# Sums of v's blocks made by accumulating transfers, two halves split in one instruction, and a row's transfers planned longer

## The chip, the cores and the metric

The kernel runs on one core of a Trainium2 chip. The metric is the device time of one execution in microseconds; lower is better. The engines of the core are named as the profile names them: PE (matrix products; PEld is its weight load), DVE (vector), ACT (scalar functions), POOL (GpSimd, here used nearly only to issue transfers), SP (issues the other transfers).

## What is computed

Channel attention followed by a layer with an activation in between. For each of 4 batches, with 6080 rows and 256 channels:

```python
qn = q / (np.linalg.norm(q, axis=1, keepdims=True) + 1e-06)
kn = k / (np.linalg.norm(k, axis=1, keepdims=True) + 1e-06)
s = kn.transpose(0, 2, 1) @ qn / tau
a = np.exp(s - s.max(-1, keepdims=True))
a /= a.sum(-1, keepdims=True) + 1e-09
x = (v @ a).reshape(24320, 256)
h = x @ w_in                          # 256 -> 2048
g = np.where(h >= 1, h, np.where(h <= -1, 0.0, (h + 1) ** 2 / 4))
out = g @ w_out                       # 2048 -> 256
```

All inputs and the output are float32.

## The kernel before

The product a @ w_in is formed once for a batch ("W", in eight pieces of 256 hidden columns), so that the bulk of the work is h = v @ W and out = g @ w_out. The rows of a batch are cut into 6 pairs of blocks of 512 (the last two pairs: 496) rows. A **group** g is one batch b, one pair k and one of the 8 pieces i; there are 192 groups, and a pair of blocks is 8 groups long. Each product of 2 x 2 blocks is made with seven block products instead of eight: for that, v's blocks (b11, b12, b21, b22) are combined into four sums, T1 = b11 + b12, T2 = T1 + b22, T3 = b12 + b22 and T4 = T2 + b21, and used beside b11, b21 and b22. Every factor is split into a high and a low half in float32r, and a product is three matmuls (`mm3`): high x high, high x low, low x high.

`make_V` makes the seven factors of a pair of blocks while the pair before it is worked on: two loads from DRAM, four additions on DVE (`combo`), and for each factor a cast to the high half (ACT, or DVE) and a subtraction for the low half (DVE). `h_ops` makes the products of a group and, in four steps of `tile_ops`, the activation: two ACT instructions and one on DVE for each of the four blocks of h, in a buffer of the pool "u". `halves_of` then splits a block into halves in a buffer of the pool "g" (tiles g and x); in a third of the groups (`o_forms`) sums of the blocks are split instead.

While a batch is worked on, the statistics for the next one are gathered. `norms` turns them into reciprocal norms in the tile cols; those of the columns are needed as a row in every partition, so SP stores them to DRAM (row_d) and loads them back, spread over all partitions, into a tile y or y_mem. `softmax` multiplies with that row on DVE, takes the exponential on ACT, transposes on PE and splits the result into halves (eT); the pieces of W are products with eT (`make_W2`).

The order of all instructions is written by the kernel's own planner (`Order`): it places operations by estimated durations, due times and free buffers, computes from that plan how late each could be, adds a table of corrections (`BIAS`) and plans again. Each engine then runs its list in that order. For transfers the planner counts a landing time:

```python
if o.size:
    dma = max(dma, t + self.DMA_BEGIN) + o.size / self.BYTES
    o.end = dma + self.DMA_END
    if o.eng == "POOL":
        o.end = max(o.end, t + self.ADDED)
```

with DMA_BEGIN 1.0, DMA_END 3.0 and ADDED 6.0 us. Accumulating transfers are used before the change for the output alone (`outT`, from tiles y and y_mem, issued by POOL).

Of the kernel before, what the change touches and what calls it, by code (L numbers as in the profile page):

```python
# [56 lines left out]
L_ADDED = 6.0  # L57
SOON = 0.6


class Op:
    __slots__ = ("eng", "dur", "fn", "due", "deps", "gates", "bufs", "next", "count", "start", "end", "n", "size",
                 "alts", "psum", "plain", "tag", "bias", "placed", "late", "freed", "latest")


class Order:
# [7 lines left out]
    DMA_BEGIN, DMA_END, ADDED = 1.0, L_END, L_ADDED  # L74

# [19 lines left out]
    def op(self, eng, dur, fn, r=(), w=(), due=0.0, gates=(), size=0, other=None, psum=False, plain=False, tag=0):  # L95
# [3 lines left out]
        o.psum, o.plain = psum, plain  # L99
# [73 lines left out]
    def plan(self):  # L173
# [25 lines left out]
        while left:  # L199
# [132 lines left out]
def dve_us(n):  # L332
    return 0.067 + 0.00104 * n
# [6 lines left out]
def pool_us(n):  # L340
# [9 lines left out]
U = 32  # L350

EARLY = 7
POOL_DMA = 1.0
T_MAX = -0.5
T_HALF = -36.2
T_FORM = -18.6
T_V = 4.5
T_VS = 29.9
T_GRAM = 34.6
T_SQ = 31.6  # L360
T_W2 = -39.4
T_O = 10.9
T_SO = 20.8
T_P4 = 3.8
BIAS = {
    (48, 4): 0.9,
    (48, 6): -1.9,
    (49, 0): 1.5,
    (49, 2): 3.8,
    (49, 5): -5.5,  # L370
    (50, 4): 1.2,
    (50, 5): -3.2,
    (51, 0, 0): -1.0,
# [12 lines left out]
    (56, 0): -4.9,
    (56, 4): -0.9,
    (62, 0): 5.3,
    (67, 0, 0, 0): -0.3,
    (67, 1, 0, 1): 0.3,  # L390
    10: 0.3,
    14: -0.2,
    15: 3.4,
    16: 0.4,
    2: 1.8,
    21: 2.8,
    27: 0.8,
    32: 6.7,
    41: 0.6,
    42: -20.7,  # L400
    46: -1.7,
    5: -4.9,
    57: 3.1,
    6: -3.5,
    65: -25.5,
    7: -2.0,
    71: 0.7,
    72: 0.2,
# [16 lines left out]
V_SPREAD = 4.2  # L425
WARM = 8
STORE = 15
IN3 = False
WIN_DUE = 21.3
W_DUE = -57.1  # L430
# [3 lines left out]
V1 = 16.2  # L434
V1S = 3.8
# [6 lines left out]
def channel_attention_moe(ctx: ExitStack, tc: tile.TileContext, kq, kqT, vT, tau, w_in, w_out, outT):  # L442
# [44 lines left out]
    def slot2(j, h):  # L487
# [16 lines left out]
        "g": Pool([sb("g6", [2, TB], F32R), *[lambda j=j, h=h: slot2(j, h) for j in range(3) for h in range(2)]]),  # L504
        "w": Pool([w_mem[:, i * WSZ:(i + 1) * WSZ].rearrange("p (a j f) -> p a j f", a=2, j=NS) for i in range(4)]),
        "v": Pool([*[sb(f"v{i}", [2, TB], F32R) for i in range(8)], *[lambda h=h: slot2(3, h) for h in range(2)]], ordered=True),
        "t": Pool([sb(f"t{i}", [TB]) for i in range(2)], ordered=True),
        "raw": Pool([*[sb(f"raw{i}", [1024]) for i in range(4)], shared.tile([P, 1024], F32, name="raw4", tag="raw")]),
        "kqs": Pool([sb("kqs", [2, RT, 2, C], F32R)]),
        "u": Pool([sb(f"u{i}", [TB]) for i in range(6)]),  # L510
# [21 lines left out]
    pools["g"].held[1:] = [kq_all] * 6  # L532
# [712 lines left out]
```

## Time and profile before

| | |
|---|---|
| time, median of 3 runs | 2140.2 us (2139.72 to 2141.19) |
| the profiled execution | 2139.28 us, its span 2137.5 us |
| busy, share of the span | PE 99%, DVE 96%, ACT 89%, POOL 8% |
| matmul instructions in the trace | 9728 |
| mean granted clock of PE | 0.998 |
| moved by the transfer engines | 386.29 MB, mean 181 GB/s |

The time of an execution holds the span, from the first to the last instruction, and a little around it. Busy time adds up an engine's instructions without counting an overlap twice. The granted clock is that of PE as a share of 2.4 GHz.

### The profile page before, as it was taken

How to read it: one execution, taken by the hardware profiler on the slowest of the kernel's cores; microseconds unless marked ns; L12 is line 12 of the kernel's file. 1: busy time of each engine (PE TensorE's matmuls, PEld its weight loads, DVE VectorE, ACT ScalarE, POOL GpSimd, SP SyncE). 2: the span in 40 equal slices, each digit the busy share in tenths (PEclk: the TensorE clock that was granted, in tenths of full speed). 3: DMA queues.
4: the chain of work that ended last, by engine and by line, in shares of the span. 5: the costliest groups of instructions: out<-in, count | busy, mean ns of one | idle time of the engine just before them, and what ended most of it. 6: DMA issues, size and time to landing. Idle time of an engine off the chain costs nothing.

```text
span 2137.5 us, 29493 instructions
## 1 busy us (share of the span) xinstructions
PE 2119.1 (99%) x9728; PEld 1764.6 (83%) x9728; DVE 2044.2 (96%) x3648; ACT 1901.5 (89%) x3530; POOL 160.5 (8%) x188
## 2 busy tenths in 40 slices
PE   9999999999999999999999999999999999999999
PEld 8888888888888888888788888888878888888887
DVE  8999999999999999999999999999989999999995
ACT  7889999998999999998898999999979899889885
POOL 0000101001001010010100101001001010010010
PEclk9999999999999999999999999999999999999999
DMA  9755657666467576665737667666564654564551
GB/s 389 277 189 187 185 185 209 193 180 157 140 213 206 193 202 203 197 182 177 169 105 243 190 204 198 193 208 189 157 166 107 208 145 128 161 145 128 160 125 37
DMA packets 108075, 386.29 MB, mean 181 GB/s; under 512 B 12050, under 2 KB 27922, under 8 KB 104082
## 3 DMA queue, kind: packets, MB, share of 16 engines
q1 hardware_dynamic: 82578, 338.73, 45.8%
q0 software_dynamic: 25344, 45.69, 15.1%
q8 instruction: 76, 1.25, 0.2%
q14 instruction: 77, 0.63, 0.1%
HBM read 280.23 MB, written 104.14 MB: 180 GB/s over the span
## 4 chain that ended last, share of the span: by engine, by line
PE 88%; DVE 7%; DMA 2%; ACT 1%; issue 1%; SPq 0%; POOL 0%; DVEq 0%; ACTq 0%; POOLq 0%
PE bank L653 88%; DVE u L934 1%; DVE x L947 1%; DVE mh_mem L1138 1%; DMA y_mem<-row_d 1%; DMA raw<-kqT 1%; DMA raw<-vT 0%; DVE w_mem L794 0%; DVE bank L970 0%; DMA y<-row_d 0%; DVE v L889 0%; DVE mh_mem L974 0%; DMA kq<-kq 0%; ACT u L930 0%; DVE u L580 0%
## 5 line engine op out<-in xcount | busy, mean ns | idle before, releaser
L653 PE MATMUL bank<-v,w_mem 128*128 128x512 f32 (+1 forms) x3240 | 854.0, 390 | 8.7 <-DVE bank L970 8.1
L653 PE MATMUL bank<-x,wout 128*128 128x512 f32 (+1 forms) x3165 | 817.0, 388 | 0.0
L653 PEld LDWEIGHTS bank<-v,w_mem 128*128 128x128 f32 x3240 | 601.9, 188 | 141.3 <-DVE bank L970 14.1
L653 PEld LDWEIGHTS bank<-x,wout 128*128 128x128 f32 x3165 | 593.6, 188 | 118.3 <-DVE x L947 0.3
L932 ACT ACTIVATE u<-u 128x512 f32<-128x512 f32 (+1 forms) x768 | 474.5, 632 | 4.3
L947 DVE TENSOR_TENSOR x<-u,x 128x512 fp32r<-128x512 f32 (+1 forms) x660 | 446.6, 687 | 4.7 <-ACT x L945 2.7
L930 ACT ACTIVATE u<-bank 128x512 f32<-128x512 f32 (+1 forms) x576 | 342.5, 595 | 89.4 <-PE bank L653 86.1
L934 DVE SCALAR_TENSOR_TENSOR u<-bank,u 128x512 f32<-128x512 f32 (+1 forms) x576 | 393.9, 686 | 21.1 <-ACT u L932 20.7
L945 ACT CAST x<-u 128x512 fp32r<-128x512 f32 (+1 forms) x461 | 283.0, 619 | 50.1 <-DVE u L934 24.4
L653 PE MATMUL bank<-x,w_mem 128*128 128x512 f32 (+1 forms) x792 | 221.2, 390 | 2.1 <-DVE cols L759 2.0
L653 PE MATMUL bank<-x,wsum 128*128 128x512 f32 (+1 forms) x645 | 178.9, 389 | 1.0 <-DVE bank L1024 1.0
L653 PEld LDWEIGHTS bank<-x,w_mem 128*128 128x128 f32 x792 | 147.0, 188 | 34.8 <-DVE cols L759 2.4
L1063 POOL DMA_DIRECT2D outT<-y_mem x88 | 79.2, 900 | 933.4 <-ACT y_mem L1093 929.6
L1063 POOL DMA_DIRECT2D outT<-y x88 | 79.1, 904 | 905.1 <-ACT y L1093 896.5
L653 PEld LDWEIGHTS bank<-x,wsum 128*128 128x128 f32 x645 | 120.4, 188 | 27.0 <-DVE bank L1024 1.7
L934 DVE SCALAR_TENSOR_TENSOR u<-mh_mem,u 128x512 f32<-128x512 f32 (+1 forms) x192 | 132.0, 687 | 9.4 <-ACT u L932 9.4
L970 DVE SCALAR_TENSOR_TENSOR bank<-bank,mh_mem 128x512 f32<-128x512 f32 (+1 forms) x192 | 133.4, 695 | 1.0 <-PE bank L653 0.4
L974 DVE SCALAR_TENSOR_TENSOR mh_mem<-bank,mh_mem 128x512 f32<-128x512 f32 (+1 forms) x192 | 131.5, 685 | 1.7 <-PE bank L653 1.5
L930 ACT ACTIVATE u<-mh_mem 128x512 f32<-128x512 f32 (+1 forms) x192 | 120.3, 627 | 7.2 <-DVE mh_mem L974 7.1
L653 PE MATMUL bank<-g,wout 128*128 128x512 f32 (+1 forms) x441 | 123.2, 388 | 0.2 <-DVE gacc L1167 0.2
L947 DVE TENSOR_TENSOR x<-t,x 128x512 fp32r<-128x512 f32 (+1 forms) x177 | 121.6, 687 | 1.5 <-ACT x L945 1.0
L965 ACT COPY mh_mem<-bank 128x512 f32<-128x512 f32 (+1 forms) x192 | 111.2, 579 | 7.8 <-DVE mh_mem L974 4.8
(137 smaller groups left out, 2405.8 us busy)
## 6 DMA issues: line engine op xcount, KB each, us to landing
w_mem<-w_d SPq DMA_DIRECT2D x160, 896.0 KB, 4.9
raw<-kqT SPq DMA_DIRECT2D x60, 512.0 KB, 5.5
w_d<-w_mem SPq DMA_DIRECT2D x32, 896.0 KB, 4.7
raw<-kq SPq DMA_DIRECT2D x55, 512.0 KB, 5.4
kq<-kq SPq DMA_DIRECT2D x18, 1024.0 KB, 10.0
raw<-vT SPq DMA_DIRECT2D x32, 512.0 KB, 5.7
outT<-y_mem POOLq DMA_DIRECT2D x60, 256.0 KB, 5.8
outT<-y POOLq DMA_DIRECT2D x60, 256.0 KB, 5.2
```

The costliest lines, as they stand in the source:

```text
L653: nc.tensor.matmul(out, lhsT=lhs(a), rhs=rhs(c), start=start and m == 0, stop=stop and m == 2, skip_group_check=skip)
L930: op("ACT", act_us(n), lambda: nc.scalar.activation(us(), src(), AF.Relu, bias=0.5, scale=0.5), r=[h], w=[u], due=d_sat, tag=(51, x, y))
L932: op("ACT", act_us(n), lambda: nc.scalar.activation(us(), us(), AF.Square), w=[u], due=d_sq, tag=(52, x, y))
L934: op("DVE", dve_us(n), lambda: nc.vector.scalar_tensor_tensor(out=us(), in0=src(), scalar=1.0, in1=us(), op0=ALU.max, op1=ALU.min), r=[h], ...
L945: op("ACT", act_us(n), lambda: nc.scalar.copy(t.ap[:, 0, :n], us()), r=[u], w=[t], due=d_hi, other=("DVE", dve1_us(n), lambda: nc.vector.t ...
L947: op("DVE", dve_us(n), lambda: nc.vector.tensor_tensor(out=t.ap[:, 1, :n], in0=us(), in1=f32(t.ap[:, 0, :n]), op=ALU.subtract), r=[u], w=[ ...
L965: op("ACT", act_us(n), lambda: nc.scalar.copy(m5.ap[:, :n], a.ap[:, :n]), r=[a], w=[m5], due=d - U, tag=57)
L970: op("DVE", dve_us(n), lambda: nc.vector.scalar_tensor_tensor(out=bb.ap[:, :n], in0=z.ap[:, :n], scalar=-1.0, in1=m5.ap[:, :n], op0=ALU.mu ...
L974: op("DVE", dve_us(n), lambda: nc.vector.scalar_tensor_tensor(out=h22.ap[:, :n], in0=z.ap[:, :n], scalar=-1.0, in1=m5.ap[:, :n], op0=ALU.m ...
L1063: op("POOL", POOL_DMA, lambda: nc.gpsimd.dma_start(out=to, in_=yb.ap[:, :m1 - m0], accum_op=ALU.add), r=[yb], w=[out_buf[c0, ct]], due=due ...
L1138: op("DVE", dve_us(1024), lambda sq=sq: nc.vector.tensor_tensor(out=acc.ap[:p], in0=acc.ap[:p], in1=sq.ap[:p], op=ALU.add), r=[sq], w=[acc ...
```

## The change

Line numbers of the changed kernel are those of its own file. Five things are done.

1. The pads. `op` and `load` get an argument `pad`, added to the planner's landing time. The row's store gets 6.0 us more and its load 3.5 us more; the new transfers of `make_V` get 2.2 us. Transfers issued in the first 60 us are counted with 1.4 instead of 3.0 us at their end.
2. `make_V` no longer adds on DVE, but for the first pair of the first batch. For each of the other 23 pairs SP loads five single blocks into the new pool "vt" (4 tiles of 512), and POOL issues four transfers that add a block from DRAM to what lies in the tile: T1, T3, then T2 on top of T1's tile, then T4 on top of that. T2 can be added only when T1's halves have been made from the tile.
3. The pools "u", "g" and "t" hold pairs (2 x 512) instead of single blocks. `halves_of` splits two blocks with one cast and one subtraction of 2x512; one factor of the groups with `o_forms` stays single (pool "g1").
4. `Bacc` is given `dynamic_dma_scratch_size=4096`; before, the argument was not given.
5. The planner's constants, due times and the table BIAS have other values.

```diff
@@ plan
-                o.end = dma + self.DMA_END
+                o.end = dma + (self.DMA_END if t > self.FIRST_LOADS else 1.4) + o.pad
                 if o.eng == "POOL":
-                    o.end = max(o.end, t + self.ADDED)
+                    o.end = max(o.end, t + self.ADDED + o.pad)
@@ norms
             op("SP", 0.45, lambda: nc.sync.dma_start(out=row_dram[b].rearrange("i p -> p i"), in_=rn()[:, CT:]), r=[c],
-               w=[row], due=due, size=1024, tag=31)
+               w=[row], due=due, size=1024, pad=6.0, tag=31)
             load(q, lambda: row_dram[b].rearrange("(o i) p -> o (i p)", o=1).broadcast_to([P, C]), lambda: q.ap[:, :C],
-                 due, 128 * 1024, r=[row])
+                 due, 128 * 1024, r=[row], pad=3.5)
@@ make_V
+        def first(x, j, h):
+            load(ts[x], lambda: blk(j, h), lambda: tt(x), due - V_AHEAD, n * 512, gates, pad=L_PAD)
+
+        def added(x, j, h, d):
+            op("POOL", POOL_DMA, lambda: nc.gpsimd.dma_start(out=tt(x), in_=blk(j, h), accum_op=ALU.add), w=[ts[x]],
+               due=due + d, gates=gates, size=n * 512, pad=L_PAD, tag=(51, x))
+
+        def direct(x, j, h, d):
+            ts[x] = buf("vt")
+            first(x, j, h)
+            summed(x, d)
...
+        first(V_T1, 0, 0)
+        added(V_T1, 1, 0, -V_AHEAD)
+        first(V_T3, 1, 1)
+        added(V_T3, 1, 0, -V_AHEAD)
+        summed(V_T1, 1)
+        direct(V_11, 0, 0, z)
+        added(V_T2, 1, 1, 1)
+        summed(V_T2, 2 * z + 1)
+        direct(V_21, 0, 1, later(V_21))
+        summed(V_T3, later(V_T3))
+        direct(V_22, 1, 1, later(V_22))
+        added(V_T4, 0, 1, 2 * z + 1)
+        summed(V_T4, later(V_T4))
@@ halves_of
-        t = gt[key] = buf("g", rank=key[0])
-        us = lambda: u.ap[:, :n]
-        op("ACT", act_us(n), lambda: nc.scalar.copy(t.ap[:, 0, :n], us()), r=[u], w=[t], due=d_hi,
+        m = len(keys)
+        t = buf("g" if m > 1 else "g1", rank=g if m > 1 else None)
+        half_ = lambda c: t.ap[:, :, c, :n] if m > 1 else t.ap[:, c, :n]
+        op("ACT", act_us(m * n), lambda: nc.scalar.copy(half_(0), src()), r=r, w=[t], due=d_hi,
...
+        op("DVE", dve_us(m * n), lambda: nc.vector.tensor_tensor(out=half_(1), in0=src(), in1=f32(half_(0)),
+                                                                op=ALU.subtract), r=r, w=[t], due=d_lo, tag=(56, keys))
@@ kernel
-    nc = bacc.Bacc("TRN2", target_bir_lowering=False, num_devices=1)
+    nc = bacc.Bacc("TRN2", target_bir_lowering=False, num_devices=1, dynamic_dma_scratch_size=4096)
```

The order that comes out differs everywhere; three places are shown. The first is DVE's list at the end of the second batch, from the reciprocal norms (line 733 before, 788 after) to the first multiplication with the row (line 754, 809). Before, 21 rows stand between the two:

```order
L733 RECIPROCAL cols_114<-cols_114 128x4
L947 TENSOR_TENSOR x_785<-u_106,x_785 128x496
L947 TENSOR_TENSOR x_680<-u_104,x_680 128x496
L946 CAST x_785<-t_96 128x496
L934 SCALAR_TENSOR_TENSOR u_108<-bank_117,u_108 128x496
...
L934 SCALAR_TENSOR_TENSOR u_106<-bank_117,u_106 128x496
L947 TENSOR_TENSOR x_680<-t_96,x_680 128x496
L947 TENSOR_TENSOR g_87<-u_109,g_87 128x496
L947 TENSOR_TENSOR x_785<-u_104,x_785 128x496
L754 SCALAR_TENSOR_TENSOR y_mem<-gacc,cols_114,y_111 128x256
```

After the change, 24 rows stand there, eight of them on 2x496 elements:

```order
L788 RECIPROCAL cols_114<-cols_114 128x4
L1091 TENSOR_TENSOR u_108<-u_108 128x496
L1034 TENSOR_TENSOR x_698<-t,x_698 128x2x496
L1091 TENSOR_TENSOR u_107<-u_107,t 128x496
L1057 SCALAR_TENSOR_TENSOR bank_117<-bank_123,mh_mem 128x496
L1034 TENSOR_TENSOR x_763<-u_108,x_763 128x2x496
...
L1021 SCALAR_TENSOR_TENSOR u_108<-mh_mem,u_108 128x496
L1033 CAST x_763<-u_108 128x2x496
L1021 SCALAR_TENSOR_TENSOR u_107<-bank_122,u_107 128x496
L1034 TENSOR_TENSOR x_763<-u_108,x_763 128x2x496
L809 SCALAR_TENSOR_TENSOR y_mem<-gacc,cols_114,y_111 128x256
```

The multiplication has moved back by three rows, and the rows ahead of it have become longer.

The second is DVE's list after the change, in the second batch, where T2 follows T1 in the same tile (vt_100): the first row makes T1's low half, the last one T2's. Between them POOL's transfer has to add b22 and a cast has to make T2's high half.

```order
L934 TENSOR_TENSOR v_88<-vt_100,v_88 128x496
L1061 SCALAR_TENSOR_TENSOR mh_mem<-bank_122,mh_mem 128x512
L1021 SCALAR_TENSOR_TENSOR u_109<-bank_116,u_109 128x512
L1034 TENSOR_TENSOR x_687<-u_107,x_687 128x2x512
L1021 SCALAR_TENSOR_TENSOR u_108<-bank_117,u_108 128x512
L1021 SCALAR_TENSOR_TENSOR u_108<-mh_mem,u_108 128x512
L934 TENSOR_TENSOR v_89<-vt_98,v_89 128x496
L1034 TENSOR_TENSOR x_698<-u_108,x_698 128x2x512
L1021 SCALAR_TENSOR_TENSOR u_109<-bank_122,u_109 128x512
L738 TENSOR_TENSOR gacc<-bank_123,gacc 128x512
L1034 TENSOR_TENSOR x_763<-u_109,x_763 128x2x512
L934 TENSOR_TENSOR v_90<-vt_100,v_90 128x496
```

Ten rows stand between the two; before the change T2 was one DVE addition ahead of its halves, with no transfer between.

The third is PE's list after the change at the same boundary, from the transposes of the softmax (line 827) to the first product with eT (tile win_mem, W's first pieces for the next batch):

```order
L827 MATMUL bank_123<-ident,y_mem 128x128 x4
L708 MATMUL bank_118<-x_698,wout 128x512 x3
L708 MATMUL bank_119<-x_698,wout 128x512 x6
L708 MATMUL bank_121<-x_687,wsum_1307 128x496 x3
L708 MATMUL bank_122<-v_89,w_mem 128x496 x3
L708 MATMUL bank_119<-g_87,wout 128x496 x3
L708 MATMUL bank_117<-v_90,w_mem 128x496 x3
L708 MATMUL bank_116<-v_95,w_mem 128x496 x3
L708 MATMUL bank_119<-x_687,wsum_1307 128x496 x3
L708 MATMUL bank_122<-v_91,w_mem 128x496 x3
L708 MATMUL bank_123<-win_mem,eT 128x512 x6
```

Nine rows stand between them; before the change 29 rows did.

## Rows read from the trace of the kernel before

**Rows 1.** The page, busy time, share of the span and instructions of each engine.

```profile
PE 2119.1 (99%) x9728; PEld 1764.6 (83%) x9728; DVE 2044.2 (96%) x3648; ACT 1901.5 (89%) x3530; POOL 160.5 (8%) x188
```

**Rows 2.** Stretches of the span (us from its start), columns in the first line.

```profile
core 0: us, PE busy (x) PEld busy (x) DVE busy (x) ACT busy (x) POOL busy (x), PEclk, DMA share, GB/s
...
400.00:450.00 50.00, 50.00 (x236) 42.23 (x235) 49.94 (x89) 47.23 (x91) 6.95 (x8) 1.00 0.78 211
...
1055.40:1058.40 3.00, 2.94 (x7) 2.44 (x8) 2.98 (x9) 0.61 (x4) 0.00 (x0) 0.50 1.00 399
1585.40:1590.80 5.40, 5.31 (x13) 4.31 (x14) 4.71 (x12) 2.36 (x5) 0.00 (x0) 0.50 0.65 254
```

**Rows 3.** PE's waits: who for whom, us in total, times, longest.

```profile
PE bank L653 <- DVE bank L970: 8.1, 5, 4.3
PE bank L653 <- DVE cols L759: 2.0, 1, 2.0
PE bank L1149 <- POOL ones L474: 1.0, 1, 1.0
PE bank L653 <- DVE bank L1024: 1.0, 1, 1.0
```

**Rows 4.** PE's timeline: start us, us, what, how many.

```profile
528.44 0.82 PE L653 MATMUL bank<-x,wout 128*128 128x496 f32 x3
...
532.07 0.83 PE L653 MATMUL bank<-v,w_mem 128*128 128x496 f32 x3
532.74 0.61 PE L653 MATMUL bank<-x,wout 128*128 128x496 f32 x2
...
1050.92 1.50 PE L653 MATMUL bank<-x,wout 128*128 128x496 f32 x6
...
1059.05 0.83 PE L653 MATMUL bank<-g,wout 128*128 128x496 f32 x3
...
1579.72 1.51 PE L653 MATMUL bank<-x,wout 128*128 128x496 f32 x6
...
1591.55 2.17 PE L653 MATMUL bank<-x,wout 128*128 128x496 f32 x9
```

**Rows 5.** DVE's timeline at the three boundaries: start us, us, what, [idle before, releaser].

```profile
510.67 0.17 DVE L733 RECIPROCAL cols<-cols 128x4 f32<-128x4 f32 x1
...
525.80 0.48 DVE L754 SCALAR_TENSOR_TENSOR y<-gacc,cols,y_mem 128x256 f32<-128x256 f32 x1 [2.58 <-DMA y_mem<-row_d]
...
1036.75 0.17 DVE L733 RECIPROCAL cols<-cols 128x4 f32<-128x4 f32 x1
...
1044.07 0.67 DVE L974 SCALAR_TENSOR_TENSOR mh_mem<-bank,mh_mem 128x496 f32<-128x496 f32 x1
1044.65 0.67 DVE L934 SCALAR_TENSOR_TENSOR u<-bank,u 128x496 f32<-128x496 f32 x1
...
1052.77 0.48 DVE L754 SCALAR_TENSOR_TENSOR y_mem<-gacc,cols,y 128x256 f32<-128x256 f32 x1 [3.96 <-DMA y<-row_d]
...
1566.23 0.17 DVE L733 RECIPROCAL cols<-cols 128x4 f32<-128x4 f32 x1
...
1582.48 0.48 DVE L754 SCALAR_TENSOR_TENSOR y<-gacc,cols,y_mem 128x256 f32<-128x256 f32 x1 [5.20 <-DMA y_mem<-row_d]
```

**Rows 6.** Transfers to and from row_d: issue to landing.

```profile
DMA to landing us min/median/max: 5.2/7.8/10.6
```

**Rows 7.** DVE groups: line, what, how many, busy us, mean ns, idle before.

```profile
L947 DVE TENSOR_TENSOR x<-u,x 128x512 fp32r<-128x512 f32 (+1 forms) x660 | 446.6, 687 | 4.7 <-ACT x L945 2.7
...
L1138 DVE TENSOR_TENSOR mh_mem<-mh_mem,y_mem 128x1024 f32<-128x1024 f32 (+1 forms) x12 | 14.7, 1227 | 8.2 <-ACT y_mem L1136 8.0
```

**Rows 8.** POOL's accumulating transfers to outT: issue ns min/median/max, and their landing.

```profile
L1063 POOL DMA_DIRECT2D outT<-y_mem x88: 865/865/1517, 238.8 to 2062.3; - x88
...
DMA to landing us min/median/max: 3.8/5.5/14.0
```

**Rows 9.** The page, transfer queues: packets, MB, share of 16 engines.

```profile
q0 software_dynamic: 25344, 45.69, 15.1%
```

More of the change, by code (lines that the diff above doesn't have):

```diff
@@ new lines @@
+T_HALF = -26.0
+T_FORM = 9.4
+T_V = 13.0
+T_VS = 5.4
+T_GRAM = 24.5
+T_SQ = 31.2
+T_W2 = -46.1
+T_O = 4.9
+T_SO = 2.7
+T_P4 = -5.7
+BIAS = {
+    (48, 0): 1.5,
+    (48, 1): 0.4,
+    (48, 2): -6.2,
+    (48, 3): 2.0,
+    (48, 4): 1.9,
+    (48, 5): 0.6,
+    (49, 1): -7.2,
+    (49, 2): 6.2,
+    (49, 4): -3.0,
+    (51, 0): -0.6,
+    (51, 2): -2.1,
+    (51, 4): -0.5,
+    (51, 6): 3.3,
+    (52, 0.8999999999999773): -1.0,
+    (52, 0.9000000000000057): -0.3,
+    (52, 0.900000000000091): 1.9,
+    (52, 12.400000000000091): 1.0,
+    (52, 2.3999999999999773): -0.1,
+    (52, 2.4000000000000057): -8.2,
+    (52, 2.400000000000091): 0.7,
+    (52, 4.400000000000006): 11.0,
+    (52, 4.400000000000091): 2.4,
+    (53, 0.8999999999999773): -5.6,
+    (53, 0.9000000000000057): -4.9,
+    (53, 0.900000000000091): 0.6,
+    (53, 12.400000000000006): 8.5,
+    (53, 12.400000000000091): -0.7,
+    (53, 2.3999999999999773): 1.0,
+    (53, 2.4000000000000057): -5.2,
+    (53, 4.399999999999977): -2.3,
+    (53, 4.400000000000006): -17.4,
+    (53, 4.400000000000091): 1.5,
+    (54, 0.8999999999999773): -1.0,
+    (54, 0.9000000000000057): 4.0,
+    (54, 0.900000000000091): -2.9,
+    (54, 12.400000000000006): 2.3,
+    (54, 12.400000000000091): -1.9,
+    (54, 2.3999999999999773): 6.5,
+    (54, 2.4000000000000057): -9.6,
+    (54, 2.400000000000091): 1.7,
+    (54, 4.399999999999977): 0.6,
+    (55, ((0, 0), (1, 0))): 2.1,
+    (55, ((0, 1), (1, 1))): 1.1,
+    (55, (6, 3)): -0.6,
+    (56, ((0, 0), (1, 0))): -0.6,
+    (56, ((0, 1), (1, 1))): 1.2,
+    (56, (0, 2)): 2.2,
+    (56, (1,)): -7.4,
+    (56, (6, 3)): 1.8,
+    (57, 0): -0.4,
+    (57, 1): 0.2,
+    (57, 2): -0.2,
+    (57, 4): -0.1,
+    (63, 1): -1.7,
+    (63, 2): 0.1,
+    (63, 5): 5.7,
+    (63, 6): -14.1,
+    (69, 0, 0, 0): 0.1,
+    (69, 0, 1, 0): -0.4,
+    (69, 1, 0, 0): 0.3,
+    1: 2.1,
+    14: 0.3,
+    15: -0.3,
+    17: 0.9,
+    18: 0.8,
+    20: 0.3,
+    21: 3.0,
+    27: -13.9,
+    3: 3.6,
+    32: 8.2,
+    35: 2.5,
+    41: 0.6,
+    42: -5.3,
+    43: -34.3,
+    44: 1.7,
+    46: -0.3,
+    5: 0.9,
+    58: -0.3,
+    6: -3.8,
+    60: -1.8,
+    64: -3.3,
+    66: 1.3,
+    7: 0.3,
+    74: 7.0,
+    77: -1.9,
+    8: -2.5,
@@ L992, in o_forms @@
         c11, c12, c21, c22 = (o_buf[b, k, y, ct] for ct in range(CT) for y in range(2))
-        u11, u12, u21, u22 = (gu[g, x, y] for x in range(2) for y in range(2))
-        t1, t2, m5 = (buf("t") for _ in range(3))
+        left, right = gu.pop(g)
+        sums = two("t")
         def plus(out, a, c, due):
-            op("DVE", dve_us(n), lambda: V.tensor_tensor(out=out.ap[:, :n], in0=a.ap[:, :n], in1=c.ap[:, :n],
-                                                         op=ALU.add),
-               r=[x for x in (a, c) if x is not out], w=[out], due=due, tag=61)
@@ new lines, in plus, with halves @@
+            op("DVE", dve_us(n), lambda: V.tensor_tensor(out=at(out), in0=at(a), in1=at(c), op=ALU.add),
+               r=[b for p, j in (a, c) for b in (p[0], p[1 + j]) if b is not out[0][1 + out[1]]] + [out[0][0]],
+               w=[out[0][1 + out[1]]], due=due, tag=62)
+        def halves(p, keys, due):
+            j = slice(None) if len(keys) > 1 else 0
+            halves_of(lambda: p[0].ap[:, j, :n], p if len(keys) > 1 else p[:2], g, keys, due, due + 1, n)
+        f = d + T_FORM
+        halves(left, (V_11,), f + 18)
```

335 lines of the change are left out of this document (149 added, 186 removed).

## Prediction

> **What bounds the kernel now.** I read the page's busy times first: TensorE (PE) is busy for 99% of the span, VectorE (DVE) for 96%, ScalarE (ACT) for 89% [rows 1]. Next I cut the span into stretches of 50 us. The one shown is typical of the steady part: PE 50.00 of 50.00 us busy, DVE 49.94, at a granted clock of 1.00 [rows 2]. So in the steady part the matmuls alone set the time, and a lighter DVE or ACT cannot shorten it. Only where PE stands still is there anything to win, and the list of PE's waits says where: 8.1 us on line 970, 2.0 us on the cols tile of line 759, 1.0 us on line 1024, and none of the others longer than the 1.0 us of the start [rows 3].
>
> In order of time, three of those stand-stills make up nearly everything [rows 4]. A 496-wide matmul starts every 0.22 us (three in 0.67 us between 532.07 and 532.74). From 528.44 to 532.07 six start: 3.63 us for 1.32 us of work, 2.31 us lost. From 1050.92 to 1059.05 fifteen start: 8.13 us for 3.30, 4.83 us lost. From 1579.72 to 1591.55 twenty-one start: 11.83 us for 4.62, 7.21 us lost. Sum **14.35 us**. In the last two the wait is only part of it: behind it the granted clock is 0.50, the lower of its two levels (1.2 GHz), for 3.0 and 5.4 us [rows 2]. In the first, after the shorter wait, no such stretch follows.
>
> Why does PE stand still? The three places are the last groups of batches 0, 1 and 2, where the softmax for the next batch is made. DVE computes the reciprocal norms (line 733), SP stores them as a row to DRAM and loads them back spread over all partitions, and DVE multiplies with them (line 754). In DVE's order of time that round trip takes 15.13 us (510.67 to 525.80), 16.02 us and 16.25 us, and DVE sits idle for the last 2.58, 3.96 and 5.20 us of it, held by the row's load [rows 5]. Its work before that, which covers the trip, is 12.55, 12.06 and 11.05 us long. Everything queued on DVE behind line 754 waits, line 970 first, and for that PE waits. The two transfers are nearly the whole trip: they land 5.2 to 10.6 us after their issue, 7.8 at the median [rows 6].
>
> **The change part by part.**
>
> *The row's pads.* The planner is told 6.0 us more for the row's store and 3.5 us more for its load, so it places line 754 (809 now) later in DVE's order. At the second boundary 21 rows stand between reciprocal and multiplication before, and 24 now, of which six are subtractions of 2x496 and two are casts of 2x496. Worked out in time: a 496-wide DVE instruction of 0.67 us lets the next start 0.58 us later [rows 5], so 0.09 us of it overlaps; one of 1024 elements takes 1.227 us [rows 7], so it holds DVE for about 1.13 us, and one of 992 for 1.10. Sixteen singles at 0.58 are 9.3, six doubles 6.6, and two double casts at 0.6 (an estimate: twice half a tensor instruction's 0.58) 1.2: **17.1 us**; the third boundary has the same rows, the first 19 singles, five doubles, two casts, 17.7 us. Against trips of 15.1 to 16.3 us the cover is now 0.8 to 2.6 us too long instead of 2.6 to 5.2 us too short. So the three stalls go, and with them the slow stretches behind two of them: −14.4 us. The lower bound is that all of it stays.
>
> *Halves as one pair.* Of 969 hi/lo subtractions of 512 on DVE 902 become 451 of twice the width. Two hold DVE for 2 x 0.60 = 1.20 us, one for 1.13 [rows 7], with the overlap above: 451 x 0.07 = 32 us less on DVE. ACT saves likewise on its casts. None of it lies on PE's path; it is slack where DVE is 99% busy [rows 2].
>
> *Sums of v's blocks by transfers.* 92 DVE additions (4 for each of 23 pairs) of the kind that takes 0.687 us [rows 7] go away: 92 x 0.60 = 55 us of DVE. The planner gives part of that back: 192 casts of twice the width and 30 single ones stand on DVE where 291 single ones stood, at 0.6 and 0.3 us some 37 us more. DVE falls from 2044 to about 1994 us. That can end the one PE wait on DVE away from the boundaries that has a row of its own, line 1024's 1.0 us; I take it whole. In their place come 92 accumulating transfers on POOL's queue. POOL is 8% busy, and an issue there takes 0.865 us [rows 8]: 80 us more for it, hidden. The software queue moved 45.69 MB in 15.1% of the DMA engines' time [rows 9]; 23.6 MB more is 7.8%, in stretches that are 78% busy [rows 2]. What counts is the wait for them. The trace has no accumulation into SBUF; the nearest row is the accumulation into DRAM: 3.8 us to land at the least, 5.5 at the median, 14.0 at most [rows 8]. T2 can only be added once T1's halves are done, T4 once T2's are. The shortest cover on DVE is the one shown below: ten rows, seven singles and three doubles, 7.6 us. The chain in it is a landing and one cast of 0.6 us: 6.1 us at the median, 4.4 at the least. So most of them are covered, and the few that land late cost a wait of 1 to 3 us, which PE sees in part. I take +1.0 us for all 23 pairs together and keep the price of late sums (below) as the far end.
>
> *Scratch of 4 KB.* The trace shows no use of that memory. It can only matter if an issue on POOL waits for an earlier one to land: T3 behind T1, 5.5 us late, is not needed before T2. I take 0, with 0 to 1 us.
>
> *Matmuls.* Both programs issue 9561 matmul instructions; 18 of the 512-wide ones become 496-wide, −0.1 us. The start-up orders its conversions differently, with the same instructions and the same bytes; ±2 us. On the last group the tail keeps its form, 0.
>
> *Sum.* −14.4 − 1.0 + 1.0 − 0.1 = −14.5, against the profiled execution's 2139.28 us (span 2137.5): 2124.8; the median of the runs shown is 0.9 us above that execution: **2125.7 us**.
>
> One rule speaks against the transfers. The row first: POOL's issues of DMAs have a median of 0.865 us and a maximum of 1.517, in a kernel whose DVE is busy for 96% of its time [rows 1, 8]. Were every new issue to take that maximum, the chain of 6.1 us would be 6.8, still under its cover of 7.6, and the sum would stay. The Trainium skill ("SBUF — State Buffer", A bandwidth-pool intuition that's wrong) has a GpSimd-issued DMA go from about 620 to about 3100 ns beside a DVE copy that holds the shared port. By that rule each sum would land some 2.2 us later than here, an estimate from the page's 3100 ns; half of the pairs would wait 0.7 us, and the time would be near 2134.
>
> **The rivals.**
>
> *The row comes back later than now.* The chain of the row is the same, but more traffic shares the DMA engines. If the trips grow to 18.5 us, DVE waits 0.8 to 1.4 us at each boundary, and PE loses about as much, 3 to 4 us without a slow clock, up to 9 with it: 2129 to 2135. For it: the cover exceeds the third trip by only 0.9 us. Against it: the DMAs issued next to the row are the same. The Trainium skill ("DMA: Bandwidth & Descriptors", Issuing engines are not separate DMA queues) says that transfers from all queues share the same 16 engines; no row here separates them.
>
> *The sums come late.* If accumulations into SBUF land like the slower ones here, at 9 us and more, the chain is 9.6 us against 7.6 to about 9 in half of the pairs. DVE or ACT then stands still for 1 to 2 us, twice for a pair, and PE loses it as it did at the boundaries, where 2.58 us on DVE cost it 2.31. At 23 x 2 x 1.1 us it is 50 us more than my sum: about 2175. It is slower than before from a mean loss of 0.67 us for each pair. Against it: they are mostly issued alone, while the DRAM ones come in bursts of four to eight.
>
> *Softmax moves too close to its user.* At the second and third boundary nine rows of PE stand between the transposes and the first product with eT, 6.7 us, where 29 stood before. The way from one to the other is three instructions of some 0.6 us. That is enough, unless ACT or DVE is behind: then PE waits there for 1 to 4 us twice, 2128 to 2133 (counted with the first rival).
>
> *The change does nothing at the bottleneck.* Fewer and larger buffers make PE wait elsewhere for what it gains at the boundaries: 2136 to 2144.
>
> **How the numbers follow.** Gone stalls, covered sums: 0.60 (its own range 2121 to 2129). Late row, late eT, or sums late by less than 1 us (the same band): 0.20 (2129 to 2136). Nothing gained: 0.08. Late sums: 0.12 (2144 to 2175). The range of 8 in 10 takes in the first two and the start-up's ±2 us: 2119 to 2138. 0.2% of the time is 4.3 us, about what a measurement tells from no change: faster 0.80, same 0.08, slower 0.12.
>
> **What would show it.** Right: at the three boundaries DVE reaches line 809 with no idle time put down to the row's load, PE shows no wait above 1 us there and the clock stays at 1.00; DVE's busy time is near 1990 us; T2's cast and subtraction have no DMA as releaser. Wrong: a wait on vt (the tile of the sums) or on the row that repeats for each pair or batch, POOL issues far above 0.9 us, or PE idle where its stretches are full now.

## The result and the profile after

The changed kernel takes **2118.8 us** at the median (2118.27 to 2119.02, four runs) beside 2139.96 us (2137.88 to 2141.19, four runs) for the kernel before on the same chip: ratio 0.9902, 95% interval 0.9885 to 0.9919. The gain is 21.2 us; predicted were 14.5. The time lies 6.9 us below the forecast of 2125.7, and 0.2 us below the range of 2119 to 2138. The profiled execution takes 2118.88 us, its span 2117.1, and PE's mean granted clock is 1.0.

On the page, the busy times, the software queue and the transfers of v's blocks (line, operation, count, KB, median us to landing):

```profile
PE 2110.0 (100%) x9728; PEld 1766.1 (83%) x9728; DVE 2001.7 (95%) x3034; ACT 1818.3 (86%) x3150; POOL 244.6 (12%) x280
...
q0 software_dynamic: 38592, 69.55, 22.5%
...
vt<-vT SPq DMA_DIRECT2D x75, 256.0 KB, 5.6
...
vt<-vT POOLq DMA_DIRECT2D x60, 256.0 KB, 4.9
```

DVE has 42.5 us less to do than in [rows 1], ACT 83 us less, and the software queue moves 23.9 MB more than in [rows 9].

The three boundaries, on DVE's timeline: the reciprocal norms, and the first multiplication with the row.

```profile
505.81 0.17 DVE L788 RECIPROCAL cols<-cols 128x4 f32<-128x4 f32 x1
...
525.34 0.48 DVE L809 SCALAR_TENSOR_TENSOR y<-gacc,cols,y_mem 128x256 f32<-128x256 f32 x1 [0.18 <-DMA y_mem<-row_d]
...
1027.52 0.17 DVE L788 RECIPROCAL cols<-cols 128x4 f32<-128x4 f32 x1
...
1047.73 0.48 DVE L809 SCALAR_TENSOR_TENSOR y_mem<-gacc,cols,y 128x256 f32<-128x256 f32 x1
...
1549.67 0.17 DVE L788 RECIPROCAL cols<-cols 128x4 f32<-128x4 f32 x1
...
1569.88 0.48 DVE L809 SCALAR_TENSOR_TENSOR y<-gacc,cols,y_mem 128x256 f32<-128x256 f32 x1
```

Where [rows 5] had 2.58, 3.96 and 5.20 us of idle time for the row, there are 0.18, 0 and 0. PE in the 10 us behind each (columns as in [rows 2]) is full and at full clock:

```profile
526.00:536.00 10.00, 10.00 (x49) 8.42 (x48) 9.68 (x19) 6.64 (x16) 1.77 (x2) 1.00 0.85 251
1048.00:1058.00 10.00, 10.00 (x47) 8.42 (x46) 9.41 (x20) 6.85 (x16) 1.75 (x2) 1.00 0.87 263
1570.00:1580.00 10.00, 10.00 (x46) 8.41 (x45) 9.41 (x20) 6.85 (x17) 1.78 (x2) 1.00 0.67 199
```

To see where all of it went I took, for each kernel, the time from the start of each matmul to the start of the next, less the usual pace of its width (227 ns for 512, 220 for 496, 120 for 256, the median for the few others). The remainder is PE's loss. Between the two profiles, 20.4 us apart in span:

| PE's loss, us | before | after | difference |
|---|---|---|---|
| first 100 us | 34.6 | 35.1 | +0.6 |
| around the boundaries (498 to 545, 1020 to 1068, 1540 to 1600) | 15.1 | 2.2 | -12.9 |
| elsewhere | 15.0 | 8.3 | -6.7 |
| matmuls at their usual pace | 2067.4 | 2066.3 | -1.1 |
| behind the last matmul's start | 4.8 | 4.5 | -0.3 |

So the boundaries gave what was expected of them, and a second gain of 6.7 us lies elsewhere. The view that shows most of it is the list of waits of PE's weight loads (PEld), which the prediction does not use. Before (us in total, times, longest):

```profile
PEld bank L653 <- DVE bank L970: 14.9, 27, 4.7
PEld bank L653 <- DVE u L934: 7.4, 32, 0.8
PEld bank L653 <- ACT bank L967: 2.5, 8, 0.4
```

And after:

```profile
PEld bank L708 <- ACT bank L1054: 3.8, 9, 1.6
PEld bank L708 <- DVE u L1021: 3.7, 11, 0.7
PEld bank L708 <- DVE bank L1119: 3.6, 14, 0.4
```

All rows of that list add up to 38.3 us in 95 waits before, and to 16.9 us in 55 after; without the first 100 us and the boundaries, to 21.0 us in 78 and 11.2 us in 42. [Rows 3], PE's own list, shows five waits for line 970; the weight loads have 27, and 32 more for line 934, most of some 0.2 us. Of the 15.0 us lost elsewhere before, six starts late by over 150 ns make 3.1, 73 late by 20 to 150 ns 5.8, and all others, by a little each, 6.0; after it is 1.2 (three), 3.8 (47) and 3.2. In 58 of the 79 late starts before, with 8.0 of their 8.9 us, a weight load waits in the time between. So some 3.9 us of the 6.7 belong to starts that are late by over 20 ns, most of them behind such a wait; for the other 2.8, a little at each of thousands of starts, no view shows a cause. The busy times don't show any of this. In the kernel before the last 500 us of the steady part read as full and lost 4.4 us, with starts up to 147 ns late (367 ns instead of 220):

```profile
1600.00:2100.00 500.00, 500.00 (x2208) 411.77 (x2208) 478.02 (x846) 440.12 (x827) 41.80 (x48) 1.00 0.52 142
```

### The profile page after: what moved, and what is told of

Read it like the earlier page. It is cut to its first block, busy times and chain, and to the rows that moved or that the text cites. A ratio compares the mean times of both kernels' runs of the same rounds, so it can differ in the third digit from the quotient of the medians.

```text
span 2117.1 us, 28614 instructions
## 1 busy us (share of the span) xinstructions
PE 2110.0 (100%) x9728; PEld 1766.1 (83%) x9728; DVE 2001.7 (95%) x3034; ACT 1818.3 (86%) x3150; POOL 244.6 (12%) x280
## 4 chain that ended last, share of the span: by engine, by line
PE 96%; DVE 2%; DMA 1%; ACT 1%; issue 0%; DVEq 0%; SPq 0%; POOL 0%; POOLq 0%
PE bank L708 93%; PE bank L1218 3%; DMA raw<-kq 0%; DMA raw<-kqT 0%; DVE u L1021 0%; DVE u L634 0%; PE bank L1245 0%; DVE x L1034 0%; DVE w_mem L849 0%; ACT u L1020 0%; ACT u L1018 0%; DVE u L625 0%; DVE wout L641 0%; DVE u L630 0%; DVE u L632 0%
## 5 line engine op out<-in xcount | busy, mean ns | idle before, releaser
L708 PE MATMUL bank<-x,wout 128*128 128x512 f32 (+1 forms) x3405 | 865.3, 388 | 0.0
L708 PEld LDWEIGHTS bank<-x,wout 128*128 128x128 f32 x3405 | 636.6, 188 | 128.7 <-DVE bank L1119 3.0
L1034 DVE TENSOR_TENSOR x<-u,x 128x1024 fp32r<-128x1024 f32 (+1 forms) x384 | 461.2, 1205 | 9.6 <-ACT x L1032 7.7
L1032 ACT CAST x<-u 128x1024 fp32r<-128x1024 f32 (+1 forms) x206 | 215.1, 1045 | 27.7 <-DVE u L1021 18.8
L970 POOL DMA_DIRECT2D vt<-vT x92 | 80.9, 903 | 1227.9 <-DMA vt<-vT 486.3
L708 PE MATMUL bank<-x,wsum 128*128 128x512 f32 (+1 forms) x804 | 221.4, 388 | 0.0
L708 PE MATMUL bank<-x,w_mem 128*128 128x512 f32 (+1 forms) x768 | 209.3, 388 | 0.0
L708 PEld LDWEIGHTS bank<-x,wsum 128*128 128x128 f32 x804 | 149.2, 188 | 28.9 <-DVE bank L1119 0.6
L1033 DVE CAST x<-u 128x1024 fp32r<-128x1024 f32 (+1 forms) x178 | 121.6, 683 | 5.8 <-PE bank L708 0.7
L1054 ACT COPY bank<-bank 128x512 f32<-128x512 f32 (+1 forms) x192 | 112.4, 585 | 8.3 <-PE bank L708 5.7
```

The costliest lines, as they stand in the source:

```text
L708: nc.tensor.matmul(out, lhsT=lhs(a), rhs=rhs(c), start=start and m == 0, stop=stop and m == 2, skip_group_check=skip)
L1032: op("ACT", act_us(m * n), lambda: nc.scalar.copy(half_(0), src()), r=r, w=[t], due=d_hi, other=("DVE", dve1_us(m * n), lambda: nc.vector. ...
L1033: other=("DVE", dve1_us(m * n), lambda: nc.vector.tensor_copy(half_(0), src())) if g >= FIRST else None, tag=(55, keys))
L1034: op("DVE", dve_us(m * n), lambda: nc.vector.tensor_tensor(out=half_(1), in0=src(), in1=f32(half_(0)), op=ALU.subtract), r=r, w=[t], due=d ...
L1054: op("ACT", act_us(n), lambda: nc.scalar.copy(a.ap[:, :n], z.ap[:, :n]), r=[z], w=[a], due=d - U, tag=59)
```

## The experiments

The kernel before was run beside each group on the same chip; its median there was between 2137.8 and 2145.2 us. The kernels without boundary stalls hardly differ between chips (the changed one took 2118.8, 2119.5 and 2117.7), so their times are compared directly, to within the 2 us by which these three differ. "Boundaries" and "elsewhere" are the losses of the table above, from each profile. For the repeats g4 and h4 2117 to 2121 and 2118 to 2120 were expected.

| kernel | median us | ratio to before (95%) | boundaries | elsewhere |
|---|---|---|---|---|
| e1 pads alone | 2126.75 | 0.9919 (0.9904 to 0.9934) | 3.0 | 14.5 |
| e2 changed, no row pads | 2139.73 | 0.9977 (0.9967 to 0.9986) | 21.5 | 8.6 |
| e3 changed, sums on DVE | 2130.54 | 0.9936 (0.9921 to 0.995) | 1.5 | 20.4 |
| e4 changed, single halves | 2124.65 | 0.991 (0.9893 to 0.9926) | 1.8 | 13.2 |
| f1 changed, no table | 2121.62 | 0.9921 (0.9905 to 0.9938) | 1.7 | 11.5 |
| f2 pads alone, no table | 2133.72 | 0.9978 (0.9969 to 0.9988) | 2.5 | 22.2 |
| f3 as e3, no table | 2132.63 | 0.9973 (0.9961 to 0.9984) | 2.1 | 21.1 |
| f4 as e4, no table | 2118.41 | 0.9905 (0.989 to 0.9919) | 1.6 | 6.6 |
| g1 as f1, idle additions planned | 2130.23 | 0.9935 (0.992 to 0.995) | 3.7 | 16.5 |
| g2 as f3, additions left out | 2126.27 | 0.9917 (0.9902 to 0.9932) | 3.7 | 12.7 |
| g3 changed, pad all on the load | 2120.07 | 0.9889 (0.9874 to 0.9904) | 2.7 | 9.3 |
| g4 changed again | 2119.49 | 0.9886 (0.987 to 0.9903) | 2.0 | 8.4 |
| h1 as e1, additions cut short | 2125.30 | 0.9912 (0.9897 to 0.9927) | 2.7 | 13.4 |
| h2 changed, unplanned additions | 2156.86 | 1.0059 (1.0044 to 1.0074) | 6.3 | 42.3 |
| h3 as f4 again | 2118.74 | 0.9883 (0.9866 to 0.9899) | 1.5 | 6.3 |
| h4 changed again | 2117.74 | 0.9876 (0.9861 to 0.9891) | 2.8 | 7.2 |
| e5 changed, no pad for v | 2132.06 | 0.9937 (0.9922 to 0.9952) | 2.2 | 21.1 |
| e7 before, small scratch | 2143.88 | 0.9999 (0.999 to 1.0009) | 19.1 | 14.5 |

### The pads, alone and taken away

```diff
 e1: the kernel before, with
-   w=[row], due=due, size=1024, tag=31)
+   w=[row], due=due, size=1024, pad=6.0, tag=31)
-   due, 128 * 1024, r=[row])
+   due, 128 * 1024, r=[row], pad=3.5)
 e2: the changed kernel, with
-   size=1024, pad=6.0, tag=31)
+   size=1024, pad=0.0, tag=31)
-   due, 128 * 1024, r=[row], pad=3.5)
+   due, 128 * 1024, r=[row], pad=0.0)
```

> The kernel before with the row's pads alone (6.0 us for the store, 3.5 us for the load), all else as before. In DVE's order 36, 41 and 34 rows now stand between the reciprocal norms and the multiplication at the three boundaries, about 19.6, 22.6 and 18.7 us of work where 12.0, 11.7 and 10.9 stood. Theory (the pads remove the boundary stalls, the rest of the gain comes from elsewhere): the three stalls go, about -14 us, time 2124 to 2128; PE's small losses away from the boundaries (15.6 us after the first 100 us in the profile before) stay as they are. Rival (the lighter DVE removes the stalls, the pads do little): 2136 to 2141.

> The changed kernel with both pads of the row at 0. In DVE's order 10 to 12 rows, 7 to 8 us of work, stand between the reciprocal norms and the multiplication. Theory: the trip takes 16 to 19 us, DVE is idle for 8 to 11 us at each boundary, PE loses about as much and works at the lower clock behind it: 25 to 40 us in all, time 2144 to 2159. Rival (a lighter DVE is what removed the stalls): 2118 to 2124.

Alone, the pads bring the kernel to 2126.75 us: the boundaries' loss falls from 15.1 to 3.0, and the loss elsewhere stays (14.5 beside 15.0). Taken from the changed kernel, they cost 20 us, less than the 25 to 40 expected: DVE waits for the row for 8.4 us at the first boundary, as expected, but for 17.7 us at all three together. The loss elsewhere stays at 8.6. In e2 DVE's wait at the first boundary, and two stretches there and one at the third (columns as in [rows 2]):

```profile
530.14 0.48 DVE L809 SCALAR_TENSOR_TENSOR y<-gacc,cols,y_mem 128x256 f32<-128x256 f32 x1 [8.45 <-DMA y_mem<-row_d]
```

```profile
523.00:531.00 8.00, 0.37 (x2) 0.00 (x0) 0.86 (x2) 1.47 (x3) 0.00 (x0) 0.67 0.78 178
531.00:536.00 5.00, 4.73 (x12) 3.86 (x13) 5.00 (x8) 1.54 (x2) 0.00 (x0) 0.50 1.00 398
...
1591.00:1594.00 3.00, 3.00 (x7) 2.44 (x8) 2.97 (x6) 1.38 (x4) 0.00 (x0) 0.50 0.88 336
```

With a DVE as light as the changed kernel's the boundaries lose 21.5 us, more than in the kernel before (15.1, and 19.1 in e7): the row's trip and its place in the order decide it, not DVE's load. The two gains are separate and add up.

### The sums of v's blocks

```diff
 e3: the changed kernel, with DVE's additions for every pair
-        if (b, k) == (0, 0):
+        if True:
             raws = [raw_buf() for _ in range(2)]
```

> The changed kernel with v's four sums added on DVE for all pairs again (two loads for a pair, no accumulating transfers into vt); pads, pairs of halves, scratch and tables as changed. DVE gets 92 additions back. Theory A (the 6 us that PE lost less away from the boundaries come from DVE's new slack, and the transfers gave most of that): 2122 to 2126, with new PE waits on DVE away from the boundaries. Theory B (the transfers give nothing on the path, the traffic of their blocks even makes the row's trip longer): 2117 to 2120, and the row's trip falls from 18.5 to 19.4 us back to 15 to 16.

2130.5: 11 to 13 us more, all of it elsewhere. That is more than theory A's 3 to 7 and rules out B (the row's trip did not get shorter either: 20.1 us at the first boundary, 21.8 at the third), though in part because the table was fitted to the other work. So the next four were run with the table emptied (`BIAS = {}`), for the changed kernel (f1), e1 (f2), e3 (f3) and e4 (f4).

> The changed kernel with the table BIAS emptied, so that the planner's order carries no corrections by hand or search. Theory A (the lighter DVE is what saves the 6 us away from the boundaries): 2121 to 2128, and at least 4 us below the same emptying of the kernel with the pads alone. Theory B (the 6 us come from the tables that were fitted to the new work): 2128 to 2140, no faster than the kernel with the pads alone and no table.

> The kernel before with the row's pads and with an empty table. Theory A: 2130 to 2142, with most of the loss in PE's waits for DVE away from the boundaries. Theory B: within 2 us of the changed kernel with no table.

> The changed kernel with v's sums on DVE and an empty table. With the changed kernel's table the sums on DVE cost 11.7 us. Theory A (the transfers save this by themselves): 5 to 12 us above the changed kernel with no table. Theory B (it is only that the table was fitted to the transfers): within 3 us of it.

The table is worth 2 to 4 us to the changed kernel and 7.0 to the one with the pads alone. Without it the sums on DVE cost 11.0 us (f3 less f1), so the transfers' gain does not hang on the table (the due times stayed). f3 and f2 differ by all of the change but the transfers and the table, and by 1.1 us. Is it DVE's time? Four runs ask that. g1 adds 92 idle additions that the planner knows; g2 has neither additions nor transfers; h1 and h2 keep the order of every engine to the row, and change only DVE's load.

```diff
 g1: f1, with four of these for each of the 23 pairs
+            op("DVE", dve_us(n), lambda: nc.vector.tensor_tensor(out=spare[:, :n], in0=spare[:, :n], in1=spare[:, :n], op=ALU.add),
+               w=[spare_buf], due=due + d, gates=gates, tag=50)
 g2: f3, halves made from single blocks, no combo(...)
 h1: e1, where b or k is not 0
-   tensor_tensor(out=tt(x), in0=a(), in1=c(), op=ALU.add)
+   tensor_tensor(out=tt(x)[:, :32], in0=a()[:, :32], in1=c()[:, :32], op=ALU.add)
 h2: the changed kernel, ahead of the low halves of T1 to T4, not in the plan
+   nc.vector.tensor_tensor(out=spare[:, :n], in0=spare[:, :n], in1=spare[:, :n], op=ALU.add)
```

> The changed kernel with no table, transfers kept, and 92 additions of no use on DVE (on a spare tile that nothing else reads, four for each of the 23 pairs at the due times of the old sums). Theory A (what the transfers save is DVE's time alone): about the time of the kernel with the sums on DVE and no table, 2128 to 2134, DVE's busy time near 2026 us. Theory C (what they save is the chain from a sum to its halves and the buffers it holds, not the load): 2120 to 2125.

> The kernel with v's blocks loaded in pairs and no table, and with the additions left out (the halves of T1 to T4 are made from single blocks, so part of the computation is missing), hence neither DVE additions nor accumulating transfers. Theory A: within 3 us of the changed kernel with no table (2121.6). If the transfers cost something of their own (late sums, traffic): 3 us or more below it. Theory C's opposite: above 2126.

> The kernel before with the pads alone, in exactly its own order on every engine, but with the 92 additions of v's blocks cut to 32 columns (so part of the sums is missing): the planner still counts them at full length. DVE loses some 45 to 50 us of work, nothing is moved and no transfer is added. Theory A (DVE's time is what the sums cost): 6 to 9 us less than with the full additions (2126.8), 2118 to 2121. Theory B' (the saving comes from the order that the planner can make without them): 2125 to 2127.

> The changed kernel in exactly its own order, with an addition of no use (512 or 496 wide, on a spare tile) put in DVE's list ahead of each low half of T1 to T4, 92 in all, that the planner knows nothing of. Theory A: 7 to 14 us more than the changed kernel (2119), 2126 to 2133. Theory B': within 2 us of it. A loss far above 14 us would mean that a plan that is too short costs more than the load itself.

g1 costs 8.6 us over f1: planned additions that feed nothing cost most of what the real ones do. That is theory A's time and not theory C's, though DVE's busy time rises by 36.6 us alone (1998.5 to 2035.1), with 75 instructions more instead of 92: the planner gives casts to ACT. g2 lies 4.7 us above f1: outside theory A's 3 us, not below f1 as a cost of the transfers would have it, and just inside the band above 2126 that was put down as theory C's opposite. Its order loses 2.5 us at 166 to 170 us and 1.4 at 517 that f1's does not. h1 is the surprise. DVE's busy time falls from 2044.1 to 2010.9 us, by less than the 45 to 50 expected but nearly to that of the changed kernel, and only 1.5 us come back. Its page, and the waits of its weight loads:

```profile
PE 2113.4 (100%) x9728; PEld 1762.7 (83%) x9728; DVE 2010.9 (95%) x3648; ACT 1899.3 (89%) x3530; POOL 161.6 (8%) x188
```

```profile
PEld bank L653 <- DVE u L935: 5.5, 26, 0.4
PEld bank L653 <- DVE bank L971: 5.4, 20, 0.9
PEld bank L653 <- ACT bank L968: 3.8, 9, 1.0
```

With the additions cut short the list comes to 27.1 us, with them at full length (e1) to 29.0. Most of the small waits stay when DVE gets lighter and the order does not change. h2 is the reverse: 92 such additions, put into a finished order directly ahead of the low halves, cost 38 to 39 us, four times what g1's cost at places that the planner chose. Its weight loads:

```profile
PEld bank L708 <- DVE bank L1124: 24.5, 45, 1.2
PEld bank L708 <- DVE mh_mem L1066: 10.8, 25, 1.4
PEld bank L708 <- DVE bank L1062: 8.7, 24, 0.9
```

Neither theory holds as it was put. A ("DVE's time") fails in h1, where less work on DVE in the same order gives 1.5 us of the 6 to 9. B' holds there, but fails in h2, where it expected 2 us and 38 came: DVE's load does cost time in a fixed order when the plan left no room for it. What fits all four runs is that most of what the transfers save is saved when the order is made, because the planner has 92 instructions fewer to fit between PE's needs. By g1 those instructions make 8.6 of the 11.0 us, by g2 6.4 (f3 less g2); whether the rest is the two "raw" buffers that a pair no longer holds, or the chance of one order against another, stays open. That chance is not small: f4 and f1, with orders of the same planner, differ by 3.2 us, and e5 (below) by 13 from the changed kernel. The gain of the transfers was seen with the table (e3) and without it (f3); that it is the 92 instructions rests on one order for g1 and one for g2.

### Halves in pairs or single

```diff
 e4: the changed kernel, for each j of the pair
-  m = len(keys); one cast and one subtraction of m * n
+  cast half_(0)[:, j], then subtraction half_(1)[:, j], each of n, due as before
```

> The changed kernel with each of the two blocks of a pair of halves cast and subtracted by an instruction of its own (width 512 or 496), in the same buffers; all else as changed. DVE gets about 30 us more work, ACT about as much. Theory A (DVE's slack is what PE gains from, the pairs give a part of it): 2121 to 2126. Theory B (the pairs are off the path): 2117 to 2120. Rival of both (single instructions give the first block's halves earlier): below 2117.

> The changed kernel with single halves and an empty table. With the changed kernel's table they cost 5.9 us. Theory A: 3 to 8 us above the changed kernel with no table. Theory B: within 3 us of it.

> The changed kernel with single halves and an empty table once more, beside the changed kernel on one chip: 2116 to 2120. If it is really better than the changed kernel it is 0.5 to 2 us below it here as well; if the first run differed only by its chip, within 0.5 us.

With the changed kernel's table single halves cost 5 to 7 us, without any table they gain 3.2 (f4 less f1), which neither theory had. The signs contradict each other, so e4 does not show what the pairs are worth. Side by side on one chip (h3, h4: 2118.74 with 2117.32 to 2119.81, 2117.74 with 2116.61 to 2118.72) the single halves lie 1.0 us above the changed kernel, with ranges that overlap: neither kind is shown to be faster. No version ran that clearly beats the changed kernel.

### The landing of the sums, the row's trip, the scratch

```diff
 e5: the changed kernel
-L_PAD = 2.2
+L_PAD = 0.0
 g3: the changed kernel; the store's pad 6.0 -> 0.0, the load's 3.5 -> 9.5
 e7: the kernel before
-   num_devices=1)
+   num_devices=1, dynamic_dma_scratch_size=4096)
```

> The changed kernel with the pad of v's transfers at 0 instead of 2.2 us (their landing is planned at 3.0 us after the load's data and 6.0 us for POOL's), table and all else kept. Accumulations into vt land 4.5 us after their issue at the median, 7.2 at the ninetieth percentile, 10.4 at most in the changed kernel. If the pad is what keeps the sums from coming late: waits of DVE or ACT on vt's transfers of 1 to 3 us in several pairs, 2121 to 2132. If 6.0 us are already enough: no such waits, 2117 to 2122 (the order shifts a little).

> The changed kernel with the row's whole pad of 9.5 us on the load and none on the store. Theory (the store's pad makes the planner issue the load later, behind other transfers and into a buffer that is still in use, so that part of the pad is used up by a longer trip): the load is issued within 0.2 us of the store's landing at all three boundaries, trips of 14.5 to 17.5 us as with no pads, DVE without a wait for the row; time within 2 us of the changed kernel, 2117 to 2121. Rival (new traffic makes the trip long): trips of 18 to 20 us as before, the load again at once behind a landing that has become later.

> The kernel before with the 4 KB scratch for dynamic transfers alone. Theory (it costs nothing with POOL's issues as they are): within 2 us of the kernel before on the same chip, POOL's issues to outT still 0.865 us at the median. Rival (a smaller scratch makes issues wait for earlier ones to land): POOL issues above 1 us, output tiles held longer, PE waits on ACT copies, 3 us or more slower.

In the changed kernel POOL's 92 accumulations into vt take this long to issue (ns min/median/max):

```profile
L970 POOL DMA_DIRECT2D vt<-vT x92: 862/872/1292, 123.9 to 2013.0; - x92
```

and the only wait of ACT or DVE for one of their tiles is this:

```profile
ACT v L931 <- DMA vt<-vT: 0.2, 1, 0.2
```

Without the 2.2 us pad (e5) there are five:

```profile
DVE v L932 <- DMA vt<-vT: 2.2, 3, 1.5
ACT x L931 <- DMA vt<-vT: 1.0, 1, 1.0
ACT v L931 <- DMA vt<-vT: 0.4, 1, 0.4
```

That is 3.6 us of direct waiting where the time rises by 13. The rest comes with an order that differs throughout. Its largest single loss is a stall of 2.2 us at 618 us, and it does not start from a sum of v: ACT, for whose line 1054 PE waits there, had stood still for 2.4 us for a block of kq, and was busy without a break from then on. Behind the stall the clock falls (621 to 625: 0.62):

```profile
613.18 1.05 ACT L717 CAST kqs<-raw 128x1024 fp32r<-128x1024 f32 x1 [2.39 <-DMA raw<-kq]
```

```profile
618.00:621.00 3.00, 0.91 (x4) 0.48 (x3) 2.79 (x6) 3.00 (x6) 0.00 (x0) 1.00 0.99 297
621.00:625.00 4.00, 4.00 (x13) 3.13 (x12) 3.96 (x6) 1.89 (x4) 0.00 (x0) 0.62 0.97 381
```

On the row's trip: from the reciprocal's start to the load's landing it took 15.0, 15.9 and 16.1 us before, and 19.4, 19.4 and 18.5 us after. In the changed kernel SP's queue at the first boundary, and what the load waits for there:

```profile
506.01 0.37 SPq L794 DMA_DIRECT2D row_d<-cols  x1
514.69 0.32 SPq L608 DMA_DIRECT2D w_mem<-w_d  x1
518.32 0.32 SPq L608 DMA_DIRECT2D y_mem<-row_d  x1
```

```profile
SPq L608 <- DMA outT<-y_mem: 3.2, 1, 3.2
```

The store has landed at 515.73 (worked out from its queue's events), but the load's tile y_mem is still being added to outT: told that the store lands late, the planner lets another user keep the tile. With the whole pad on the load (g3) it is issued at once at the first boundary, 0.07 us behind the landing, and the trips are 16.9, 17.8 and 16.6 us, the second a little over the expected 14.5 to 17.5:

```profile
505.73 0.37 SPq L794 DMA_DIRECT2D row_d<-cols  x1
516.26 0.32 SPq L608 DMA_DIRECT2D y<-row_d  x1
516.67 4.57 SPq L608 DMA_DIRECT2D w_mem<-w_d  x2
```

So at the first boundary the pad on the store holds the load up by 2.6 us. At the other two it does not: SP's queue waits there for the store itself (4.3 and 2.7 us), at the third the load follows the landing by 0.15 us, and g3's trips are shorter by 1.7 and 1.9 us because its load lands in 4.4 and 5.5 us instead of 6.6 and 7.3. With the pads alone (e1) the load is issued 1.7, 2.9 and 3.9 us behind the store's landing at the three boundaries, each time with a wait for a transfer to outT from its tile. The time stays (2120.07, beside 2119.49 for g4): PE no longer depended on it. e7 shows that the scratch costs the kernel before nothing: 0.9999 of before, POOL's issues at 0.865 us as in [rows 8]. With the changed kernel's 92 issues more it was not run apart.

## Why the prediction was right and wrong

**The row's pads, right.** Predicted were -14.4, from the profiled 2139.28 to 2124.9; the pads alone gave 2126.75 (2127.43 in the profiled execution), with 12 us gone at the boundaries, and the clock stayed at 1.00. The cover was put at 17.7, 17.1 and 17.1 us and came out at 19.4, 20.2 and 20.2: the rows were counted rightly, but DVE also sits idle for 0.9, 2.6 and 2.6 us among them, for ACT and PE. That was luck, since the trip grew as well, to 19.4, 19.4 and 18.5 us, the length that the first rival named. It cost 0.18 us of DVE and nothing of PE, because cover and trip grew together.

**Sums by transfers, wrong in size.** This is the step that failed: "the one PE wait on DVE away from the boundaries that has a row of its own, line 1024's 1.0 us; I take it whole". The term was -1.0, with +1.0 for late sums against it; elsewhere measured -6.7, and the transfers, with the pairs and tables that go with them, are worth 7 to 9 us beside the pads alone (e1), the transfers by themselves 11 with no table. The error is in the view. [Rows 3] counts waits that PE's matmuls see; 78 waits of the weight loads away from the boundaries, for lines 934, 967, 970 and others, stand in rows of their own. That in the steady part "a lighter DVE or ACT cannot shorten it", read from a stretch with PE 50.00 of 50.00 us busy, does not follow, since starts up to 147 ns late left the busy time at 500.00 of 500.00. For work taken off DVE in a fixed order the 1.0 was nearly right (h1: 1.5); what it left out is that the planner writes a new order. That the new order is what gains has g1 and g2 behind it, one order each, and for 2.8 of the 6.7 us the cause stays open.

**Late sums, right to be left near zero.** The +1.0 was 0: one wait of 0.2 us. The rival of late sums did not occur. Without the 2.2 us of pad some sums do come late, in five waits of 3.6 us; that the time is then 2132 is in part another order's. The prediction weighed the pads of the row and passed over this one.

**Halves as pairs 0, scratch 0, tail 0, not contradicted.** The runs on the pairs contradict each other in sign; e7 shows the scratch at nothing in the kernel before, and the loss behind the last matmul's start moved by 0.3 us. The start-up's +0.6 lies in its ±2. The matmuls gave -1.1 and not -0.1: 36 matmuls of 128 columns start at a median of 112 ns from one to the next instead of 138.5. Both traces hold 9728 matmuls, not the 9561 of the prediction.

**The rule against the transfers.** POOL's new issues take 0.872 us at the median and 1.292 at most, with DVE busy for 95% of the span. The Trainium skill ("SBUF — State Buffer", A bandwidth-pool intuition that's wrong) has a GpSimd-issued DMA go from about 620 to about 3100 ns beside a DVE copy; no row here comes near that. Eleven of the 92 issues overlap a cast on DVE, and they take 0.905 us at the median, 0.980 at most.

## What to carry to other kernels

A stall for a round trip is settled by the order, not by the load of the engine that waits: give the planner the trip's measured length, and check the trip again afterwards, for it moves. A pad on the first transfer of a chain can let its successor's buffer go to another user, as it did at the first boundary here; moving it to the last took that delay away there and brought no time. An engine that is "99% busy" can hide dozens of waits of 0.2 us: add up the waits of its weight loads, and the starts against the usual pace, before calling its stretches full. Where a planner writes the order, cost an instruction with the plan made again; cut short in a fixed order 92 additions were worth 1.5 us, put into one 38.

## What the runs showed of the hardware

A stall costs more than itself, and by how much varies: the first boundary's stall of 2.2 us in the kernel before left the clock at 1.00, while with the same code and small scratch (e7) it was 4.0 us long and eight matmuls behind it started every 413 ns instead of 220, at a granted clock of 0.50, the lower of its two levels (e7, columns as in [rows 2]):

```profile
535.00:536.00 1.00, 1.00 (x4) 0.83 (x3) 1.00 (x4) 0.38 (x1) 0.00 (x0) 0.50 0.00 0
```

This fits the spread of the kernel before, from 2141.1 to 2149.3 us in 13 runs on one chip, beside that of e1, without the stalls, from 2126.1 to 2127.4 in four; but only one execution of each has a trace. The gain of the changed kernel was 21 us on one chip and 25 to 27 on two others. Accumulating transfers into SBUF (256 KB) landed 4.9 us after their issue at the median, sooner than the same size into DRAM in the same kernel (6.3 to 6.5).
